# The order of the first 196 tasks of a fused conditioned-block kernel

## The chip, the cores and the metric

The kernel runs on one core of a Trainium2 chip. The metric is the device time of one execution in microseconds (us): lower is better. A core has five engines that run side by side, each through its own list of instructions in order: PE (TensorE, matrix products), ACT (ScalarE), DVE (VectorE), POOL (GpSimd) and SP, which here does nothing but issue transfers. PEld in a profile is PE's loading of weights, DMA stands for the 16 DMA engines that move the data.

## The reference

A block with adaptive layer norm, linear attention ("hedgehog" features) and a gated MLP, on 2048 tokens of width 512, in bfloat16:

```python
mod = (_silu(c) @ w_mod)                     # six vectors of 512: sa, ca, ga, sb, cb, gb
h = _layernorm(x) * (1 + ca) + sa
qkv = h @ wqkv                               # 32 heads of 16
pq, pk = q @ w_phi, k @ w_phi                # a 16x16 matrix per head
phi_q = concat(softmax(pq), softmax(-pq));   phi_k likewise
kv = sum_s phi_k v;  z = sum_s phi_k
o = (phi_q kv) / (phi_q z + 1e-6)
x = x + ga * (o @ wo)
h = _layernorm(x) * (1 + cb) + sb
x = x + gb * ((sigmoid(h @ w_gate) * (h @ w_up)) @ w_down)      # width 1376
```

## The kernel before

The tokens are 16 tiles of 128. The kernel describes its whole work as some 1230 named tasks with their data dependences; each has one engine, or a choice of engines. A text, `ORDER`, names all tasks in the order in which they are emitted, with `@A`, `@D` or `@P` where a task is to run on ACT, DVE or POOL instead of the first engine of its choices. Every engine's list of instructions is this text, filtered for the engine. `arrange` walks the text once and gives each buffer (PSUM banks, tiles of x normalised, exponentials) the place that has been free the longest; a task that gets a place waits for the last reader of what stood there before. There is no scheduler at run time.

The names that matter here. `t` is a token tile, `g` a group of the first layer norm (group 0 is tile 0, group 1 tile 1, group 2 tiles 2 and 3, group 3 tiles 4 and 5, and so on), `j` a quarter of the width:

- `ld_x0a` ... `ld_wmm2`: loads, all issued by SP. `ld_x..` are token tiles, `ld_wk..` the key weights, `ld_wv0` the value weights, `ld_wm00a` ... `ld_wm01b` the modulation weights of sa and ca, `ld_wmga` those of ga, and `ld_wmm2` (L556, 1.5 MB) those of sb, cb and gb.
- `wqT0` to `wqT3` (L669): loads of a quarter of the query weights that transpose on the way. `xT1_t` (L736): the same from SBUF to SBUF for tiles 10 to 13.
- `warm..` (L600): products of zeros, whose result nobody reads, that keep PE at work; `warm0` has six, each of the others one.
- `c1`, `c2`, `c3`: the silu of c. `modc1.h` (L630, PE) and `modc1ch` (L635 on ACT or L638 on DVE): sa and ca by halves, product and copy. `modca` (L616, from `ld_wmga`): ga. `modc2.0`, `modc2.1` (L616, PE, from `ld_wmm2`): sb, cb and gb.
- `tpw`, `wTc`, `fold1k`, `foldc1k`: the key weights are transposed on PE, copied, multiplied by w_phi (L679) and copied again (L685), so that keys come out as features' arguments; `fold0k`, `foldc0k` the same for the queries, from `wqT`.
- `st1_t` (DVE), `rs1_g` (ACT as Ln and Exp, L709 and L710, or POOL, L712 and L713), `nmr1_g` (DVE, L718), `xn1_t` (POOL L731, ACT L727, tile 0 DVE L729): the first layer norm. `tphgj` (PE, L744) transposes a quarter, `hm1_gj` (ACT L751, DVE or POOL L753) modulates it on its way out of PSUM.
- `Kta`, `Ktb`, `Vta`, `Vtb`, `Qt` (PE, L817, L821, L871): products for keys, values, queries; `et`, `qet` (ACT, L776): exponentials; `nt` (DVE, L780): sums; `rt`: reciprocals (ACT as Ln and Exp, L794 and L795, or DVE, L798); `phit` (POOL or DVE, L787); `vat` (ACT or DVE, L836); `kvt` (PE, L282): adds the tile to the sums over the tokens.

The attention and the MLP follow in the same text. SP issues a load when it comes to it in its list; each load carries one of eight semaphores, and a load waits for the landing of the one eight places ahead.

Of the kernel before, what the change touches and what calls it, by code (L numbers as in the profile page):

```python
# [43 lines left out]
modc1c1 st1_8 ld_x3a warm1_8 K1a hm1_23 xn1_5 xn1_4 tph12 nmr1_6 st1_9 hm1_03@A hm1_13@A hm1_02@A ld_wv0 wqT3 xn1_10 xn1_11 rs1_5@P K0a K0b tph31 hm1_42@A
warm1_9 hm1_12@A hm1_22@A tph32 e0.0 K3a tph30 K3b hm1_30@A ld_wmga K1b tph33 warm1_10 tph40 st1_14 st1_15 st1_13 hm1_31@A hm1_32 wqT0 e3.0 wqT1 K2b hm1_40
nmr1_5 rs1_8@P n0.0 nmr1_8 hm1_33 e2.0 V0a V1a fold03 xn1_9 xn1_8 V1b V0b e1.0 n2.0 V2a V2b tph50 hm1_50 warm1_11 xn1_15 xn1_14 n1.0 V3a wqT2 fold00 fold01
tph43 r0.0@A va1 va0 phi0.0 foldc03 fold02 foldc01 foldc02 n3.0 st1_12 foldc00 xT1_10 xT1_11 r2.0 va2@D ld_wmm2 modca.0 modca.1 hm1_60@P hm1_63@P hm1_62@P
tph82 hm1_82@A r3.0@A modcac r1.0@A phi2.0@D phi1.0@D V3b K4a K4b rs1_7@P Q0 Q2 kv0.0 Q1 qe0.0 va3 qe2.0 hm1_43@A qe1.0 modc2.0 tph52 modc2.1 tph51 nmr1_7
xn1_12 xn1_13 phi3.0@D ld_wo qn0.0 modc2c e4.0 kv1.0 qn2.0 hm1_52 kv2.0 Q4 K5a kv3.0 xT1_12 xT1_13 qphi0.0@P qphi0.1@P qn1.0 qe4.0 qphi2.1 tph80 K5b hm1_80@A
hm1_51@A e5.0 pT0 qphi2.0 n4.0 r4.0@A qn4.0 n5.0 phi4.0@D qphi1.1@P hm1_61@P qphi1.0@P tph53 V5 K7a V4 va5 hm1_53@A V6 pT2 hm1_70@P qphi4.1 va4 hm1_71 mask4  # L50
va6 K6a K7b K6b e6.0 K8 tph83 hm1_83 r5.0 qphi4.0@P e8.0 pT1 pT4 ld_wd2 tph81 hm1_81 n6.0 n8.0 e7.0 n7.0 V7 kv4.0 hm1_72@P K11 K9 V9 K14 V8 r6.0@A e9.0 va7
va9 r7.0@A e11.2 e11.6 phi5.0 phi6.0 hm1_73@P n9.0 r9.0@A kv5.0 gwa gra gwb e11.4 e14.0 K10 phi7.0@D kv6.0 K12 V10 kv7.0 e14.4 r8.0 n11.6 n11.2 r11.6 phi9.0
e10.0 e12.0 ld_wd ld_wu0 grb n11.4 n14.0 r11.2 n14.4 r14.0 n10.0 r14.4@A phi8.0 va8 V11 V14 n12.0 e11.0 K13 n11.0 phi11.6 r11.4 wo1 r11.0 va10 r10.0@A va11
kv8.0 kv9.0 phi11.2@D phi11.0@D phi10.0@D phi11.4@D V12 K15 e13.0 wmod_free ld_wg0 phi14.4 phi14.0 kv10.0 kv11.4 kv11.6 Q6 kv11.0 e13.4 r12.0@A e15.4 n13.0
n13.4 r13.0 r13.4 n15.4 e15.0 va14 V15 V13 qe6.0 va12 kv11.2 n15.0 r15.0 r15.4@A va13 phi13.4 Q5 phi15.4 phi13.0@D va15 phi15.0@D phi12.0@D wo0 wo3 Q3 kv12.0
kv13.0 kv14.0 kv15.0 qn6.0 kvn0 kvz0 kv13.4 kv14.4 kv15.4 kvz1 kvn1 num0a num1a num2a wo2 rd0a wo_all rd1a qe3.0 u0a num0b num4a num1b rd0b Q11 qe5.0 rd2a u0b
u2a rd4a num2b qn3.0 u1a rd1b tpo0 Q8 qphi6.0@P qphi6.1@P oT0 out0 num4b rd2b u1b wd0 qe11.0 u2b qphi3.1@P qphi3.0@P x1_0 rd4b st2_0 qe8.0 Q7 qe7.0 tpo1 oT1
Q10 Q9 out1 Q15 oT2 rs2_0 qn5.0 nmr2_0 xn2_0 u4a u4b x1_1 qn7.0 tsw xnT0 out2 qphi5.1@P qphi5.0@P pT6 mod02 mod00 qphi7.0@P pT3 mod03@A mod01@A qe15.0
qphi7.1@P Q13 g0.8 x1_2 tg0.8 g0.1 st2_1 wd1 rs2_1 tg0.1 u0.8 u0.1 g0.0 num3b g0.4 hm0.1 hm0.8 pT5 qe9.0 tg0.4 g0.9 wd2 u0.4 u0.9 rd3b u3b tg0.9 g0.5 num3a
hm0.4 hm0.9 u0.2 u0.0 num6a tg0.5 tg0.0 rd3a u3a u0.5 g0.2 hm0.0 hm0.5 rd6a nmr2_1 qe10.0 tg0.2 oT4 g0.10 u0.10 wd6 hm0.2 g0.3 pT7 tg0.3 u6a g0.6 num6b u0.3  # L60
y0.0 y0.1 rd6b tg0.10 hm0.10 hm0.3 num5a num5b u6b rd5b wd3 wd4 wd5 oT3 oT6 xn2_1 qe13.0 tg0.6 rd5a y0.2 u5b g0.7 tg0.7 out4 u5a oT5 qn11.0 u0.6 u0.7 xnT1
num7a hm0.6 hm0.7 mod13@A mod12@A rd7a x1_4 y0.3 out3 qphi11.1@P qphi11.0@P x1_3 st2_3 out6 mod10@A mod11@A g1.2 tg1.2 g1.1 tg1.1 num7b wd7 u1.3 u1.2 hm1.2
u7a g1.4 u1.1 y0.4 rd7b hm1.1 u1.4 y0.5 tg1.4 hm1.4 g1.0 g1.10 u1.10 g1.3 u7b st2_2 rs2_2 tg1.10 tg1.3 hm1.10 hm1.3 pT11 out5 tg1.0 u1.7 g1.7 x1_6 nmr2_2 u1.0
hm1.0 g1.5 u1.5 x1_5 qn10.0 wd8 y0.6 g1.6 oT7 xn2_2 xn2_3 g1.8 y0.7 Q14 y0.8 wd10 tg1.7 tg1.5 hm1.5 out7 u1.8 u1.6 st2_4 tg1.6 xnT2 xnT3 wd9 x1_7 qphi10.0 Q12
hm1.7 st2_6 mod21@P mod20@P qphi10.1@P y1.0 pT10 tg1.8 mod22@A mod23@A hm1.6 g1.9 y1.1 y1.2 tg1.9 u1.9 y0.9 y1.3 y1.4 g2.5 y0.10 g2.6 st2_5 qe12.0 st2_7 hm1.8
qn9.0 tg2.5 qe14.0 rs2_4 hm1.9 rs2_3 nmr2_4 y1.5 u2.0 g2.1 g2.0 tg2.0 xn2_7@D hm2.0 nmr2_3 fin0 y1.6 g2.2 tg2.2 u2.6 u2.2 hm2.2 u2.1 num11b y1.7 g2.4 rd11b
u11b xn2_6@P xnT7 xnT6 u2.5 tg2.1 xn2_5 qphi9.1@P hm2.1 tg2.6 u2.8 xn2_4 hm2.5 g2.3 num11a rd11a u11a u2.9 qphi9.0@P xnT5 y1.8 xnT4 tg2.4 u2.4 hm2.4 hm2.6
tg2.3 g2.9 u2.3 hm2.3 g2.8 tg2.8 tg2.9 u2.7 mod41@P mod43@P mod32@P mod42@P mod31@P qn13.0 g2.10 hm2.8 g2.7 y1.9 num10a qn8.0 num10b y2.0 y1.10 tg2.7 hm2.7
rd10a hm2.9 qphi8.0@P u2.10 pT9 y2.1 y2.2 y2.3 y2.4 y2.5 qn14.0 num9b rd9b qphi13.0 qphi8.1@P mod30@A mod33@A tg2.10 mod40@A y2.6 y2.7 g3.3 wr qphi13.1@P
tg3.3 oT11 g3.0 u10a rd10b u10b pT8 oT10 hm2.10 qn15.0 g3.8 num9a rd9a u9a u3.0 out11 y2.8 g3.1 y2.9 qphi14.1 fin1 x1_11 u9b u3.3 hm3.3 st1 tg3.8 tg3.0 u3.8  # L70
num8a st2_11 num8b rd8b rd8a u8a pT13 qphi15.0 hm3.8 u8b u3.9 g3.4 u3.2 out10 x1_10 qphi14.0 oT8 oT9 hm3.0 st2_10 y2.10 g3.6 u3.6 qn12.0 rs2_6 out8 tg3.4
# [987 lines left out]
```

## Time and profile before

| What | Value |
|---|---|
| Time, median of 3 runs | 205.37 us (205.24 to 207.14) |
| Profiled execution: span from first to last instruction | 203.3 us |
| Outside the span, median less span | 2.1 us |
| Share of the span busy: PE, PEld, DVE, ACT, POOL | 96%, 52%, 79%, 52%, 50% |
| Mean granted PE clock | 1.00 |
| HBM read, written | 11.58 MB, 2.10 MB |

Of the profiled execution the page gives the span; what its whole time has beside the span is read from the median of the runs. A line of a profile in order of time has the start in us, the duration, engine, line of the kernel, operation, output and inputs by name, and how often it came in a row; in brackets, how long the engine had been idle and what ended that. SPq is SP's queue, where an issue is shown with the time that it took. The chain of waits is the work that ended last, followed backward.

### The profile page before, as it was taken

To read this page: it belongs to the slowest core of one execution; us is meant where nothing else is said; L and a number is where in the kernel's file an instruction comes from. 1 tells how busy PE (TensorE), PEld (TensorE's weight loads), DVE (VectorE), ACT (ScalarE), POOL (GpSimd) and SP (SyncE) were. 2 spreads that over 40 slices of the span, in tenths; PEclk is the share of its full clock that TensorE was granted. 3 is DMA by queue.
4 is the path that set the end of the run, shared out by engine and by line. 5 is a ranking of instruction groups with operands and counts; after the bars stand their busy time and mean duration, and the time that the engine had idled before them with its cause. 6 is when DMAs were issued, how large, how long until landed. Compare 5 with 4: busy or idle time off the path is not lost.

```text
span 203.3 us, 4138 instructions
## 1 busy us (share of the span) xinstructions
PE 194.9 (96%) x1447; PEld 106.7 (52%) x1471; DVE 160.6 (79%) x374; ACT 105.9 (52%) x257; POOL 102.1 (50%) x143
## 2 busy tenths in 40 slices
PE   7789999999999999999999999999999999999993
PEld 2455655555464687668844444444444444444442
DVE  3899999999999999999897797794969844326633
ACT  2799999999978984556451115212113311324100
POOL 4698977789689999767670056230030324000000
PEclk9999999999999999999999999999999999999999
...
GB/s 172 331 329 182 233 264 102 123 82 280 400 213 43 146 102 55 94 37 106 125 59 103 51 54 103 101 83 77 26 26 69 13 79 31 40 13 7 50 55 55
DMA packets 49453, 22.94 MB, mean 113 GB/s; under 512 B 38065, under 2 KB 47634, under 8 KB 49426
## 3 DMA queue, kind: packets, MB, share of 16 engines
...
HBM read 11.58 MB, written 2.10 MB: 67 GB/s over the span
## 4 chain that ended last, share of the span: by engine, by line
PE 75%; DVE 8%; ACT 4%; DMA 4%; issue 4%; POOL 3%; SPq 0%; POOLq 0%; DVEq 0%
PE y_ps L485 19%; PE u_ps L447 18%; PE g_ps L447 17%; PE a_ps L356 5%; DMA wmod_sb<-in_w_mod_dram 4%; PE k_ps L817 3%; PE warm L600 3%; DVE ks L780 3%; PE num L326 2%; POOL phi L787 2%; PE q_ps L871 2%; PE v_ps L821 2%; PE g_ps L449 1%; ACT h1T L751 1%; DVE qks L780 1%
## 5 line engine op out<-in xcount | busy, mean ns | idle before, releaser
L457 ACT ACTIVATE tg<-g_ps 128x512 bf16<-128x512 f32 (+5 forms) x66 | 28.8, 455 | 66.7 <-PE g_ps L447 39.5
L468 DVE SCALAR_TENSOR_TENSOR wmod_sb<-tg,u_ps 128x512 bf16<-128x512 bf16 (+4 forms) x63 | 30.3, 492 | 18.0 <-ACT tg L457 11.3
L485 PE MATMUL y_ps<-wd_sb,wmod_sb 128*128 128x512 bf16 (+4 forms) x180 | 44.2, 366 | 0.2
L447 PEld LDWEIGHTS <-wg_sb 128*128 128x128 bf16 (+1 forms) x252 | 21.9, 99 | 16.1 <-issue 0.2
L447 PEld LDWEIGHTS <-wu_sb 128*128 128x128 bf16 (+1 forms) x252 | 21.8, 99 | 16.0 <-issue 0.3
L784 POOL TENSOR_TENSOR qphi<-qe,qks 128x512 bf16<-128x512 bf16 x24 | 25.1, 1063 | 3.9 <-DMA pT<-qphi 1.0
L485 PEld LDWEIGHTS <-wmod_sb 128*128 128x128 bf16 (+1 forms) x187 | 17.1, 98 | 16.0 <-issue 0.6
L447 PE MATMUL u_ps<-wT_sb,wu_sb 128*128 128x512 bf16 (+2 forms) x124 | 23.8, 322 | 0.1
L447 PE MATMUL g_ps<-wT_sb,wg_sb 128*128 128x512 bf16 (+2 forms) x122 | 23.0, 321 | 0.2
L447 PE MATMUL g_ps<-wqk_sb,wg_sb 128*128 128x128 bf16 (+4 forms) x127 | 19.9, 286 | 0.1
L447 PE MATMUL u_ps<-wqk_sb,wu_sb 128*128 128x128 bf16 (+4 forms) x127 | 19.8, 286 | 0.2
L492 DVE TENSOR_TENSOR ot<-y_ps,x 128x512 bf16<-128x512 f32 (+2 forms) x17 | 11.1, 654 | 10.5 <-PE y_ps L485 10.4
L780 DVE TENSOR_REDUCE qks<-qe 128x64 bf16<-128x1024 bf16 x16 | 19.2, 1204 | 0.0
L780 DVE TENSOR_REDUCE ks<-e 128x64 f32<-128x1024 bf16 (+2 forms) x22 | 19.1, 905 | 0.0
L376 POOL TENSOR_SCALAR ve<-mv 128x2 f32<-128x2 f32 (+1 forms) x8 | 1.8, 226 | 34.2 <-DVE mv L366 34.1
L776 ACT ACTIVATE e<-k_ps 128x512 bf16<-128x512 f32 (+2 forms) x44 | 17.7, 504 | 0.1
L776 ACT ACTIVATE qe<-q_ps 128x512 bf16<-128x512 f32 x32 | 17.3, 608 | 0.8 <-POOL phi L787 0.4
L787 POOL TENSOR_TENSOR phi<-e,kr 128x1024 bf16<-128x1024 bf16 (+2 forms) x10 | 14.5, 1454 | 3.9 <-ACT kr L795 2.1
L817 PE MATMUL k_ps<-wqk_f,h1T 128*128 128x512 bf16 x61 | 15.9, 379 | 0.1
L356 PE MATMUL a_ps<-wo_sb,oT 128*128 128x512 bf16 x60 | 15.9, 379 | 0.2
L871 PE MATMUL q_ps<-wqk_f,h1T 128*128 128x512 bf16 x60 | 15.7, 379 | 0.2
L821 PE MATMUL v_ps<-wv_sb,h1T 128*128 128x512 bf16 x62 | 15.5, 379 | 0.0
...
## 6 DMA issues: line engine op xcount, KB each, us to landing
...
x_sb<-in_A_x_dram SPq DMA_DIRECT2D x6, 256.0 KB, 4.9
...
wu_sb<-in_B_w_up_dram SPq DMA_DIRECT2D x1, 1376.0 KB, 11.0
...
wmod_sb<-in_w_mod_dram SPq DMA_DIRECT2D x4, 256.0 KB, 6.0
wqk_sb<-in_A_wqkv_dram SPq DMA_DIRECT2D x2, 256.0 KB, 4.5
```

The costliest lines, as they stand in the source:

```text
L356: pe.matmul(ap_[:], lhsT=oT[:, j, :], rhs=wo_sb[:, j, :], start=(j == 0), stop=(j == KT - 1))
L447: pe.matmul(ps[:fsz, 0:n], lhsT=w[:, j, ft * P:ft * P + fsz], rhs=h[:, j, 0:n], start=(j == 0), stop=(j == KT - 1))
L457: G.add(f"tg{k}.{ft}", {"ACT": 0.13 + n * 0.00083}, lambda e, tg=tg, g_ps=g_ps, fsz=fsz, n=n: act.activation(tg[:fsz, 0:n], g_ps[:fsz, 0:n ...
L468: dve.scalar_tensor_tensor(hm_all[:fsz, hm[k].slot, ft, 0:n], tg[:fsz, 0:n], 1.0, u_ps[:fsz, 0:n], op0=ALU.add, op1=ALU.mult)
L485: mm = pe.matmul(y[:, 0:c1 - c0], lhsT=hm_all[:fsz, hm[k].slot, ft, tl * P:(tl + 1) * P], rhs=wd_sb[:fsz, ft, c0:c1], start=(ft == 0), sto ...
L776: act.activation(ee[:, a:b, s].rearrange("p g f h -> p g (f h)"), kp[:, a * 64:b * 64].rearrange("p (g n) -> p g n", n=64), ACT.Exp, scale ...
L780: dve.tensor_reduce(ks[:, a:b].rearrange("p g s h -> p (g s) h"), ee[:, a:b].rearrange("p g s f h -> p (g s) h f"), axis=AX.X, op=ALU.add)
L784: engine(e).tensor_tensor(ph[:].rearrange("p (g s f h) -> p g s f h", s=2, f=DH, h=4)[:, :, s], ee[:, :, s], ks[:, :, 1 - s].unsqueeze(2). ...
L787: engine(e).tensor_tensor(ph[:, a * P:b * P].rearrange("p (g f h) -> p g f h", f=DH, h=4), ee[:, a:b].rearrange("p g s f h -> p (g s) f h" ...
L817: pe.matmul(kp[:], lhsT=h1T[:, j, t * P:(t + 1) * P], rhs=wqk_f[:, j, D:2 * D], start=(j == 0), stop=(j == KT - 1))
L821: pe.matmul(vp[:], lhsT=h1T[:, j, t * P:(t + 1) * P], rhs=wv_sb[:, j, :], start=(j == 0), stop=(j == KT - 1))
L871: pe.matmul(qp[:], lhsT=h1T[:, j, t * P:(t + 1) * P], rhs=wqk_f[:, j, 0:D], start=(j == 0), stop=(j == KT - 1))
```

## The change

The text `ORDER` is changed up to `V3b`, the second half of the value product of tile 3: the first 196 tasks stand in another order, and 19 of them run on another engine. From `V3b` on, all 1034 tasks stand as they did, on the same engines. No task is added or taken away. The first two lines of the text:

```diff
-pmem ld_x0b wdz warm0 c1 warm1_0 warm1_1 bd st1_2 st1_3 warm1_2 warm1_3 c2 rs1_2 ld_x0a ld_wk0 warm1_4 tpw0 st1_0 rs1_0 wTc0 st1_1 ld_wk1 rs1_1 c3 xn1_0
-nmr1_1 nmr1_2 ld_x1b st1_6 st1_7 tpw1 tpw3 wTc3 wTc1 tpw2 fold10 foldc10 wTc2 ld_wm00b ld_x1a ld_wm00a tph00 fold11 fold13 rs1_4 foldc13 fold12 foldc12 xn1_3
...
+wdz pmem warm0 ld_x0a st1_1 rs1_1 st1_0 c1 c2 ld_x0b warm1_0 warm1_1 warm1_2 warm1_3 ld_wk0 ld_wk1 nmr1_1 xn1_1@A st1_3 warm1_4 st1_2 rs1_0 xn1_0 tph11 tpw1
+tpw0 ld_x1b ld_x1a wTc1 warm1_5 tpw2 ld_wm00b c3 tph10 tph03 tph00 st1_7 tpw3 bd rs1_2@P tph13 wTc0 nmr1_2 xn1_3 xn1_2 warm1_6 ld_wm00a st1_6 wTc2 st1_4 st1_5
...
```

The 19: `rs1_2` and `rs1_4` go from ACT to POOL and `rs1_6` from POOL to ACT; `xn1_1` from POOL to ACT; `hm1_21`, `hm1_23`, `hm1_32`, `hm1_40` and `hm1_50` from DVE to ACT, and `hm1_00`, `hm1_03`, `hm1_22` and `hm1_42` from ACT to DVE; `modc1c1` from ACT to DVE; `r0`, `r1` and `r3` from ACT to DVE and `r2` from DVE to ACT; `va2` from DVE to ACT. Tile 0 and 1 are now normalised ahead of tiles 2 and 3. All twelve single fillers `warm1_..` stand ahead of the first key product; before, four of them stood behind it.

SP's list, from the last small modulation load to the big one (`wmod_sb` 128x4x1536 is `ld_wmm2`, `wT_sb` are the `wqT`, `h1T` the two `xT1`), as one piece of the difference:

```order
 L537 DMA x_sb<-in_A_x_dram 128x2x512
+L669 DMA_TRANSPOSE wT_sb<-in_A_wqkv_dram 128x4x128
 L537 DMA x_sb<-in_A_x_dram 128x4x512
 L551 DMA wv_sb<-in_A_wqkv_dram 128x4x512
 L669 DMA_TRANSPOSE wT_sb<-in_A_wqkv_dram 128x4x128
 L555 DMA wqk_sb<-in_w_mod_dram 128x4x512
-L669 DMA_TRANSPOSE wT_sb<-in_A_wqkv_dram 128x4x128 x3
+L669 DMA_TRANSPOSE wT_sb<-in_A_wqkv_dram 128x4x128 x2
 L736 DMA_TRANSPOSE h1T<-xn 128x4x128 x2
 L556 DMA wmod_sb<-in_w_mod_dram 128x4x1536
```

One of the four transposing loads of the query weights (`wqT1`) now stands ahead of `ld_x3a`, `ld_wv0` and `ld_wmga`; the other loads ahead of `ld_wmm2` change places in pairs only.

ACT's list from the first copies of transposed key weights to the first modulated tiles. Before:

```order
L664 COPY wT_sb<-tp_w 128x4x128
L709 ACTIVATE ve_83<-mv_82,eps 128x1
L710 ACTIVATE rs_84<-ve_83 128x1
L664 COPY wT_sb<-tp_w 128x4x128 x2
L685 CAST wqk_f<-fold_ps 128x512
L664 COPY wT_sb<-tp_w 128x4x128
L709 ACTIVATE ve_83<-mv_82,eps 128x2
L710 ACTIVATE rs_84<-ve_83 128x2
L685 CAST wqk_f<-fold_ps 128x512 x3
L635 COPY modc<-modc_ps 128x2
L636 ACTIVATE modc<-modc_ps 128x2
```

Of the change:

```order
L709 ACTIVATE ve_83<-mv_82,eps 128x1
L710 ACTIVATE rs_84<-ve_83 128x1
L576 ACTIVATE c_ps<-c_ps 128x4
L727 ACTIVATE xn<-x_sb,nmr,rs_84 128x512
L664 COPY wT_sb<-tp_w 128x4x128 x4
L685 CAST wqk_f<-fold_ps 128x512 x4
L635 COPY modc<-modc_ps 128x2
L636 ACTIVATE modc<-modc_ps 128x2
```

The four copies (`wTc`) and the four casts (`foldc1`) now each follow one another with no layer-norm task between them, and `xn1_1` stands ahead of them.

ACT's list at the end of the changed part, from the value copies or the last sums of the keys to `qe0.0`, the first exponential of a query (L776 `qe`). Before:

```order
L836 CAST vaug_111<-v_ps 128x32x16
L685 CAST wqk_f<-fold_ps 128x512 x4
L751 ACTIVATE h1T<-tp_h,modc 128x256
L794 ACTIVATE ks<-ks 128x64
L795 ACTIVATE kr<-ks 128x64
L648 COPY gcol<-modc_ps 128x4
L794 ACTIVATE ks<-ks 128x64
L795 ACTIVATE kr<-ks 128x64
L776 ACTIVATE qe<-q_ps 128x8x64 x2
```

Of the change:

```order
L685 CAST wqk_f<-fold_ps 128x512 x2
L836 CAST vaug_111<-v_ps 128x32x16
L836 CAST vaug_112<-v_ps 128x32x16
L794 ACTIVATE ks<-ks 128x64
L795 ACTIVATE kr<-ks 128x64
L751 ACTIVATE h1T<-tp_h,modc 128x256 x2
L776 ACTIVATE qe<-q_ps 128x8x64 x2
```

One reciprocal (`r2`) is left there instead of two, with one value copy (`va2`) and one `hm1` more; the casts of the folded query weights stand further apart.

More of the change, by code (lines that the diff above doesn't have):

```diff
@@ L44 @@
[L44 to L71, printed above, removed]
@@ new lines @@
+tpw0 ld_x1b ld_x1a wTc1 warm1_5 tpw2 ld_wm00b c3 tph10 tph03 tph00 st1_7 tpw3 bd rs1_2@P tph13 wTc0 nmr1_2 xn1_3 xn1_2 warm1_6 ld_wm00a st1_6 wTc2 st1_4 st1_5
+wTc3 fold11 fold10 warm1_7 foldc11 ld_x2b fold13 warm1_8 st1_11 foldc10 fold12 warm1_9 foldc13 modc1.0 warm1_10 ld_wm01b tph20 foldc12 warm1_11 rs1_4@P nmr1_4
+ld_wm01a modc1c0 hm1_11@A hm1_10@A tph02 rs1_3@P tph01 tph23 hm1_20@A hm1_01@A st1_10 tph21 hm1_21@A hm1_00 modc1.1 modc1c1@D rs1_6 nmr1_3 tph22 tph12 ld_x2a
+wqT1 hm1_22 hm1_13@A hm1_03 xn1_7 K1a K0a hm1_02@A hm1_23@A xn1_6 tph42 tph40 xn1_5 hm1_40@A st1_8 tph41 ld_x3a xn1_4 K3a hm1_42 hm1_12@A ld_wv0 nmr1_6 tph43
@@ new lines @@
+K3b hm1_41@A xn1_11 tph30 xn1_10 st1_9 rs1_5@P hm1_30@A tph31 wqT3 tph32 K1b ld_wmga st1_15 st1_14 hm1_31@A fold01 foldc01 K0b tph33 wqT2 rs1_8@P K2a K2b
+hm1_33 nmr1_5 V0a wqT0 V0b V3a xn1_9 e3.0 V1a xT1_11 e0.0 fold03 n3.0 V1b nmr1_8 xn1_14 va0 e2.0 n0.0 st1_13 r0.0 modca.0 modca.1 xn1_15 st1_12 xn1_8 foldc03
+n2.0 modcac e1.0 hm1_32@A V2a fold02 phi0.0 n1.0 r1.0 fold00 V2b foldc02 foldc00 r3.0 va1 xT1_10 hm1_60@P ld_wmm2 va2 r2.0@A hm1_62@P tph82 hm1_82@A tph50
+phi2.0@D phi1.0@D hm1_50@A hm1_63@P V3b K4a K4b rs1_7@P Q0 Q2 kv0.0 Q1 qe0.0 va3 qe2.0 hm1_43@A qe1.0 modc2.0 tph52 modc2.1 tph51 nmr1_7 xn1_12 xn1_13
@@ new lines @@
+rd6b tg0.10 hm0.10 hm0.3 num5a num5b u6b rd5b wd3 wd4 wd5 oT3 oT6 xn2_1 qe13.0 tg0.6 rd5a y0.2 u5b g0.7 tg0.7 out4 u5a oT5 qn11.0 u0.6 u0.7 xnT1 num7a hm0.6
+hm0.7 mod13@A mod12@A rd7a x1_4 y0.3 out3 qphi11.1@P qphi11.0@P x1_3 st2_3 out6 mod10@A mod11@A g1.2 tg1.2 g1.1 tg1.1 num7b wd7 u1.3 u1.2 hm1.2 u7a g1.4 u1.1
+y0.4 rd7b hm1.1 u1.4 y0.5 tg1.4 hm1.4 g1.0 g1.10 u1.10 g1.3 u7b st2_2 rs2_2 tg1.10 tg1.3 hm1.10 hm1.3 pT11 out5 tg1.0 u1.7 g1.7 x1_6 nmr2_2 u1.0 hm1.0 g1.5
+u1.5 x1_5 qn10.0 wd8 y0.6 g1.6 oT7 xn2_2 xn2_3 g1.8 y0.7 Q14 y0.8 wd10 tg1.7 tg1.5 hm1.5 out7 u1.8 u1.6 st2_4 tg1.6 xnT2 xnT3 wd9 x1_7 qphi10.0 Q12 hm1.7
```

51 lines of the change are left out of this document (34 added, 17 removed).

## The prediction

> **What bounds the kernel now.** I read the page's totals first, then the busy time by stages, then the chain of waits, then each engine's instructions in order of time around the place where the change ends.
>
> ```profile
> span 203.3 us, 4138 instructions
> PE 194.9 (96%) x1447; PEld 106.7 (52%) x1471; DVE 160.6 (79%) x374; ACT 105.9 (52%) x257; POOL 102.1 (50%) x143
> 10.00:15.00 5.00, 4.29 (x59) 2.78 (x60) 4.83 (x17) 4.86 (x16) 4.68 (x9) 1.00 1.14 330
> 15.00:20.00 5.00, 4.95 (x31) 2.50 (x30) 4.62 (x16) 5.00 (x13) 4.39 (x9) 1.00 1.38 182
> 66.00:200.00 134.00, 133.00 (x891) 72.54 (x904) 99.68 (x233) 47.77 (x102) 49.33 (x67) 1.00 0.34 65
> ```
>
> The columns of a stage are its length and the busy time of PE, PEld, DVE, ACT and POOL, then PE's clock, the share of the DMA engines and GB/s. PE is taken from 15 us to the end (4.95 of 5, 133 of 134). A busy PE need not be a PE at its peak, so I looked at the spacing: a product of 512 columns follows the last one at 0.216 us.
>
> ```profile
> 33.35 0.86 PE v_ps L821 x4
> ```
>
> Four such products in 0.86 us is what every full row of PE between 16 and 200 us shows. So behind the head the kernel is one dense row of PE work in a fixed order, and its end moves with the moment at which PE gets through the head. In the tail nothing is reordered. The question is only: when does PE get past the seam, and what holds it there?
>
> ```profile
> 21.41 7.44 DMA wmod_sb<-in_w_mod_dram
> 28.90 0.82 PE modc_ps L616 x24
> ...
> 24.37 0.59 PE L821 MATMUL v_ps<-wv_sb,h1T 128*128 128x512 bf16 x2
> 27.65 1.02 PE L871 MATMUL q_ps<-wqk_f,h1T 128*128 128x512 bf16 x3
> 28.90 0.75 PE L616 MATMUL modc_ps<-sc_bf,wmod_sb 128*128 128x1 bf16 x22 [0.22 <-DMA wmod_sb<-in_w_mod_dram]
> ```
>
> The first two lines are of the chain of waits, the others of PE in order of time. The changed part ends with V3b at 24.37 (the first task that stays). From there PE runs K4, Q0, Q2, kv0 and Q1; Q1 starts at 27.65 and its four products end at 27.65 + 4 x 0.216 = 28.51 (one record is missing). Then comes modc2.0, which reads the 1.5 MB load wmm2. That load was issued at 21.41 and landed 7.44 us later, at 28.85; modc2.0 starts at 28.90. **PE has 0.39 us of true waiting there, and the chain leaves the engines for the DMA.** This load is the gate between head and tail.
>
> **The change part by part.**
>
> *PE reaches the gate earlier.* In the kernel before, four of the fillers (warm1_8 to warm1_11) stand behind the first key product; now all stand ahead of it. That takes 4 x 0.216 = 0.86 us out of the dense part.
>
> ```profile
> 10.30 0.55 PE L630 MATMUL modc_ps<-sc_bf,wmod_sb 128*128 128x1 bf16 x16
> 13.56 0.54 PE L630 MATMUL modc_ps<-sc_bf,wmod_sb 128*128 128x1 bf16 x16
> 14.20 0.38 PE L817 MATMUL k_ps<-wqk_f,h1T 128*128 128x512 bf16 x1
> 5.63 2.08 SPq L542 DMA_DIRECT2D wmod_sb<-in_w_mod_dram  x2
> wmod_sb<-in_w_mod_dram SPq DMA_DIRECT2D x4, 256.0 KB, 6.0
> 10.48 1.54 ACT L685 CAST wqk_f<-fold_ps 128x512 bf16<-128x512 f32 x3
> 11.90 0.18 ACT L635 COPY modc<-modc_ps 128x2 f32<-128x2 f32 x1
> 12.19 2.42 ACT L751 ACTIVATE h1T<-tp_h,modc 128x128 bf16<-128x128 bf16 x6
> 14.48 0.18 ACT L635 COPY modc<-modc_ps 128x2 f32<-128x2 f32 x1
> ```
>
> The first key product stands at about 14.0 (14.20 is the second of the pair). modc1.0 is done at 10.85, but ACT copies the modulation columns only at 11.90, because three copies of folded weights go first, from 10.48 on. In the new order ACT has the four weight casts behind it by about 10.7: xn1_1 has come to it (I take 0.6 us, as one of its 512-column casts above), one rs task less stands ahead, and its copies of the transposed weights run without a break. So the modulation copy can start at 10.95, 0.95 us earlier. The second modulation product, at 13.5 so far behind other PE work, then runs when its weights land: the last of the two issues from 5.63 starts at about 6.7, and 6.0 us later is 12.7. Its columns go to DVE now, and with 0.6 us for the product, the copy and one hm1 the first key product comes at about 13.6. PE arrives at the gate 0.4 + 0.86 = 1.26 us earlier, at **27.3** instead of 28.51.
>
> *ACT and DVE at the seam.* From the first modulation copy (11.90) to qe0.0 (26.73) ACT is full for 14.83 us.
>
> ```profile
> 18.01 1.06 ACT L751 ACTIVATE h1T<-tp_h,modc 128x256 bf16<-128x256 bf16 x2
> 18.90 3.09 ACT L776 ACTIVATE e<-k_ps 128x512 bf16<-128x512 f32 x6
> 21.77 0.37 ACT L794 ACTIVATE ks<-ks 128x64 f32<-128x64 f32 x1
> 22.34 1.06 ACT L836 CAST vaug<-v_ps 128x512 bf16<-128x512 f32 x2
> 23.28 2.06 ACT L685 CAST wqk_f<-fold_ps 128x512 bf16<-128x512 f32 x4
> 26.73 1.08 ACT L776 ACTIVATE qe<-q_ps 128x512 bf16<-128x512 f32 x2
> 28.10 0.33 DVE L718 TENSOR_SCALAR nmr<-mv,rs 128x1 f32<-128x1 f32 x2
> 38.68 0.41 DVE L753 TENSOR_SCALAR h1T<-tp_h,modc 128x256 bf16<-128x256 bf16 x1 [0.38 <-PE tp_h L744]
> ```
>
> Prices are from start to start: an hm1 of two tiles 0.45 (18.01 to 18.90 for two), of one tile 0.35 (six mixed ones from 12.19 to 14.48 take 2.29), a reciprocal as Ln and Exp 0.57 (21.77 to 22.34), a value copy 0.47 (22.34 to 23.28 for two). In that stretch ACT gains five wide hm1 (21, 23, 32, 40, 50), one rs (0.44), r2 and va2, and gives up two wide (22, 42) and two narrow (00, 03) hm1, modc1c1 (0.29) and r0, r1, r3: 3 x 0.45 - 2 x 0.35 + 0.44 - 0.29 - 2 x 0.57 + 0.47 = +0.1. With some 0.2 of new short waits ACT is at qe0.0 at 10.95 + 14.83 + 0.3 = 26.1 to 26.2, 0.5 earlier. DVE does the mirror image of it (a net of about zero) and loses the waits that it has ahead of 20 us; I put its seam (28.10) 0.4 earlier. POOL gets two rs tasks for one rs and one xn, about even. None of the three reaches the seam late, and none of the leads is worth much: DVE waits 0.38 us for PE at 38.68 in any case.
>
> *The gate itself.* This term decides. The queue of loads holds the same transfers ahead of wmm2; wqT1, a transposing load, goes from behind the ga weights to a place ahead of x3a, and wv0, wqT3 and the ga weights each start one transfer later.
>
> ```profile
> 10.47 1.78 SPq L669 DMA_TRANSPOSE wT_sb<-in_A_wqkv_dram  x1
> 12.92 5.08 SPq L669 DMA_TRANSPOSE wT_sb<-in_A_wqkv_dram  x3
> 18.12 3.23 SPq L736 DMA_TRANSPOSE h1T<-xn  x2
> 14.54 3.03 POOL L731 TENSOR_SCALAR xn<-x_sb,rs,nmr 128x512 bf16<-128x512 bf16 x4
> 17.00:18.00 1.00, 1.00 (x9) 0.54 (x7) 0.97 (x4) 1.00 (x3) 0.92 (x3) 1.00 1.15 349
> 18.50:19.00 0.50, 0.50 (x7) 0.37 (x6) 0.41 (x2) 0.50 (x3) 0.42 (x3) 1.00 0.01 1
> 19.00:19.50 0.50, 0.50 (x6) 0.25 (x3) 0.34 (x2) 0.50 (x3) 0.50 (x1) 1.00 0.08 9
> 22.50:23.00 0.50, 0.45 (x3) 0.24 (x3) 0.50 (x3) 0.50 (x2) 0.50 (x2) 1.00 0.88 74
> 24.00:25.00 1.00, 1.00 (x18) 0.66 (x16) 1.00 (x2) 1.00 (x3) 1.00 (x2) 1.00 1.05 418
> ```
>
> SP is full from 10.47 to 21.98: issuing is the pace, and the transposes take 1.3 to 1.8 us each. The last two, xT1_10 and xT1_11, read what POOL finished at 14.54 + 3.03 = 17.57, ahead of 18.12, so they did not wait for data; in the new order I get the same two xn at about 17.2. So the work ahead of wmm2 is the same on SP and on the DMA engines, and I take its landing as unchanged: **28.85, term 0**. The bounds: below, the issue could come so early that the hole around 22.5 to 23.5 closes (74 GB/s against 418 later; 1.0 us at a fifth of the rate is 0.8 us): -0.8. Above, a transpose among plain loads can leave a hole as at 18.5 to 19.5, where 1 and 9 GB/s moved: +1.0, and wqT1 now stands alone among plain loads, so one more such place exists. Zero lies between the two.
>
> [...]
>
> *Late loads inside the head.* x3a and wv0 land later by about one transpose, which I put at 1 us (4 transposes and two plain loads fill SP from 10.47 to 18.0). V0a would come at 18.2 and wv0 at 17.5 to 18; fold02 and fold00 may wait up to 0.8 us for wqT2 and wqT0. The 1.55 us between 27.3 and 28.85 cover that.
>
> *The sum.* At the gate: max(27.3, 28.85) = the same 28.85 as now. PE's lead of 1.26 us turns into a longer wait for the load, 1.55 instead of 0.39 us. Behind it one other wait can shrink a little by DVE's lead:
>
> ```profile
> 58.57 0.93 PE L326 MATMUL num<-kvb,pT 128*128 128x68 bf16 x24 [0.36 <-DVE kvb L299]
> ```
>
> I give it 0.1 us. The profiled span would be 203.3 - 0.1 = 203.2. The median of the timed runs, 205.37, lies 2.1 above the profiled span; with that the forecast is **205.3 us**. A difference under 1% (2.05 us) is about what a measurement of this kernel cannot tell from no change.
>
> **The rivals.**
>
> *The load lands earlier (faster).* If SP gets to wmm2 early enough, the gate moves to 28.05, and if the holes between transposes go too, down to PE's own 27.3. For it: the holes are there. Against: SP is full, and nothing is taken off it. Time: 205.3 - 0.8 to 205.3 - 1.55, so 203.8 to 204.5. PE's own arrival is a floor, so a gain of over 1% would need PE's head to shrink by more than I find. [...]
>
> *The load lands later (slower).* The lone transpose ahead of x3a leaves a hole of its own and the three behind keep theirs. Each us of delay behind 28.85 costs one us of the whole, since PE is dense after it: one hole, 1.0 us, gives 206.3; two give 207.3. It is slower from the first tenth that wmm2 lands behind 28.85, and over 1% from 30.9 on. For it: the 1 GB/s at 18.5 begins where a plain load gives way to transposes. Against: between 10 and 15 us the engines moved 330 GB/s with small packets too.
>
> *The clock.* PE ran its first fillers at half rate:
>
> ```profile
> 4.11 2.31 PE L600 MATMUL warm<-wd_sb 128*128 128x512 bf16 x5
> ```
>
> Five in about 2.1 us is 0.43 each, though the clock column says 1.00. Were PE to fall back to that between 10.8 and 13.6 because fillers moved ahead, each product behind would take 0.43. The slack of 1.55 us covers seven such products, at 0.216 more each; fourteen, a stretch of 6 us, would cost 3.0 - 1.55 = 1.5 and give 206.8. [...]
>
> **How the numbers follow.** Gate unchanged within 0.6 us: 0.66 (204.7 to 205.9). Load earlier: 0.14. Load later: 0.15. Clock, or a head that is late for a reason I have not priced: 0.05. The range that holds eight of ten takes in most of both load rivals: 203.9 to 206.8. Faster by over 1% (under 203.3) needs PE's floor to be wrong: 0.04. Slower by over 1% (over 207.4) needs two holes or a late head: 0.07. The rest, 0.89, is the same.
>
> **What would show it.** In the changed profile: modc2.0 still ends a wait for wmm2 on PE, starting at 28.3 to 29.5; Q1's products end about 1.2 us earlier than 28.51, at 27.0 to 27.9; the first modulation copy on ACT stands near 11.0; qe0.0 near 26.2; no filler behind the first key product; wmm2 issued at 20.8 to 21.9. If PE reaches modc2.0 after the load has landed, my head is wrong; if the load lands outside 28.0 to 29.9, my term 0 is; if the two agree and the time still differs by over 1%, then the tail isn't a rigid row of PE work, and that reading is wrong.

## The result and the profile after

| | Before | After |
|---|---|---|
| Time, median | 205.41 us (17 executions) | 204.08 us (17 executions) |
| Ratio, 95% interval | | 0.992 [0.9898, 0.9942] |
| Profiled execution: span | 203.3 us | 202.6 us |

The change makes the kernel 0.8% faster: 204.08 us lies in the range of 203.9 to 206.8, but the forecast was no change, at 205.3, and the interval excludes that. A ratio leaves out executions more than 1.5% above the fastest of their kernel (one of 714.59 us among them); medians and counts below take all but that one.

The changed kernel, from the page (totals, the chain by engine) and from PE in order of time:

```profile
span 202.6 us, 4159 instructions
PE 69%; DVE 14%; ACT 6%; issue 3%; POOL 3%; DMA 3%; SPq 1%; DVEq 0%; POOLq 0%
...
13.22 0.55 PE L630 MATMUL modc_ps<-sc_bf,wmod_sb 128*128 128x1 bf16 x16 [0.48 <-ACT h1T L751]
13.84 1.02 PE L817 MATMUL k_ps<-wqk_f,h1T 128*128 128x512 bf16 x4
...
26.75 1.02 PE L871 MATMUL q_ps<-wqk_f,h1T 128*128 128x512 bf16 x4
27.68 0.82 PE L616 MATMUL modc_ps<-sc_bf,wmod_sb 128*128 128x1 bf16 x24
```

modc2.0 (L616) starts at 27.68 instead of 28.90 and no longer ends a wait for the DMA; wmm2 has left the chain. SP's queue shows why, and one group row gives the time from issue to landing:

```profile
9.28 1.51 SPq L669 DMA_TRANSPOSE wT_sb<-in_A_wqkv_dram  x1
12.01 1.62 SPq L669 DMA_TRANSPOSE wT_sb<-in_A_wqkv_dram  x1
14.30 3.07 SPq L669 DMA_TRANSPOSE wT_sb<-in_A_wqkv_dram  x2
17.49 3.13 SPq L736 DMA_TRANSPOSE h1T<-xn  x2
20.67 0.58 SPq L556 DMA_DIRECT2D wmod_sb<-in_w_mod_dram  x1
wmod_sb<-in_w_mod_dram SPq DMA_DIRECT2D x1, 1536.0 KB, 6.8
```

The six transposing loads take SP 1.51 + 1.62 + 3.07 + 3.13 = 9.33 us; before they took 1.78 + 5.08 + 3.23 = 10.09. wmm2 is issued 0.74 us earlier, about as much. (SP's other issues differ too, but nearly cancel: it is done with the last small modulation load 0.64 us later, at 8.35, and the plain loads behind that take 0.72 us less.) It lands 6.84 us later, at 27.51 (before: 28.85), while Q1's products end at 27.61. **The load came 1.34 us earlier and PE 0.90 us; now PE is the later of the two.**

From there the tail doesn't keep all of it: modc2.0 is 1.22 us earlier, the sums over the tokens from 45 us on 0.9, the span 0.7. And the medians differ by more than the spans, 1.33 us. Both differences needed an explanation.

### The profile page after: what moved, and what is told of

The parts are those of the page before. It is cut to its first block, busy times and chain, and to the rows that moved or that the text cites. A ratio compares the mean times of both kernels' runs of the same rounds, so it can differ in the third digit from the quotient of the medians.

```text
span 202.6 us, 4159 instructions
## 1 busy us (share of the span) xinstructions
PE 195.7 (97%) x1471; PEld 106.2 (52%) x1471; DVE 160.4 (79%) x375; ACT 106.1 (52%) x252; POOL 102.8 (51%) x144
## 4 chain that ended last, share of the span: by engine, by line
PE 69%; DVE 14%; ACT 6%; issue 3%; POOL 3%; DMA 3%; SPq 1%; DVEq 0%; POOLq 0%
PE y_ps L485 19%; PE u_ps L447 18%; PE g_ps L447 17%; DVE ks L780 7%; PE a_ps L356 6%; DMA wqk_sb<-in_A_wqkv_dram 3%; PE num L326 2%; DVE kr L798 2%; ACT qe L776 2%; DVE phi L787 2%; PE q_ps L871 1%; PE g_ps L449 1%; ACT h1T L751 1%; DVE qks L780 1%; POOL phi L787 1%
## 5 line engine op out<-in xcount | busy, mean ns | idle before, releaser
L485 PE MATMUL y_ps<-wd_sb,wmod_sb 128*128 128x512 bf16 (+4 forms) x187 | 45.7, 367 | 0.0
L492 DVE TENSOR_TENSOR ot<-y_ps,x 128x512 bf16<-128x512 f32 (+2 forms) x17 | 11.1, 654 | 10.2 <-PE y_ps L485 10.1
L776 ACT ACTIVATE e<-k_ps 128x512 bf16<-128x512 f32 (+2 forms) x44 | 18.2, 522 | 0.0
L776 ACT ACTIVATE qe<-q_ps 128x512 bf16<-128x512 f32 x32 | 17.4, 618 | 0.6 <-POOL phi L787 0.4
L817 PE MATMUL k_ps<-wqk_f,h1T 128*128 128x512 bf16 x64 | 16.5, 379 | 0.0
L821 PE MATMUL v_ps<-wv_sb,h1T 128*128 128x512 bf16 x64 | 16.1, 379 | 0.1
```

Source lines behind the costliest of these rows:

```text
L485: mm = pe.matmul(y[:, 0:c1 - c0], lhsT=hm_all[:fsz, hm[k].slot, ft, tl * P:(tl + 1) * P], rhs=wd_sb[:fsz, ft, c0:c1], start=(ft == 0), sto ...
L776: act.activation(ee[:, a:b, s].rearrange("p g f h -> p g (f h)"), kp[:, a * 64:b * 64].rearrange("p (g n) -> p g n", n=64), ACT.Exp, scale ...
L817: pe.matmul(kp[:], lhsT=h1T[:, j, t * P:(t + 1) * P], rhs=wqk_f[:, j, D:2 * D], start=(j == 0), stop=(j == KT - 1))
L821: pe.matmul(vp[:], lhsT=h1T[:, j, t * P:(t + 1) * P], rhs=wv_sb[:, j, :], start=(j == 0), stop=(j == KT - 1))
```

## The experiments

### Load order and fillers, one at a time

Two rivals to "the gate opens at the later of PE and the load": the load alone carries the gain, or PE's head and the moved engines do. Each of the two parts was put alone into the kernel before, then both, and the load was put back in the changed kernel.

The load alone:

```diff
-ld_x3a ... ld_wv0 wqT3 ... ld_wmga ... wqT0 e3.0 wqT1
+wqT1 ld_x3a ... ld_wv0 wqT3 ... ld_wmga ... wqT0 e3.0
```

> The kernel before with one task moved: the transposing load wqT1 ahead of ld_x3a, nothing else. Theory M (the gate opens at the later of two arrivals, PE's and the load's): the 1.5 MB load wmm2 is issued about 20.7 instead of 21.41 and lands at 27.5 to 28.1 instead of 28.85; PE's own arrival stays at 28.51, so modc2.0 starts at about 28.55 with no wait for the load, and the time is 0.3 to 0.4 us lower: about 205.0 against 205.4. Rival L (the load alone carries the gain): 1.3 us lower, 204.1. Rival P (PE's head and the engines alone carry it): no change, 205.4.

The fillers alone (twelve as before, the last four now behind tph00, fold13 and tph11):

```diff
-tph00 fold11 fold13 ... tph11 ... warm1_5 ... warm1_6 ... warm1_7 ... K2a ... warm1_8 K1a ... warm1_9 ... warm1_10 ... warm1_11
+tph00 warm1_5 warm1_6 fold11 fold13 warm1_7 ... tph11 warm1_8 ... warm1_9 ... warm1_10 ... warm1_11 ... K2a ... K1a
```

> The kernel before with only the four fillers that stand behind the first key product moved ahead of it, into PE's waits between 7.8 and 11.6 us; loads and engines as they were. Theory M: Q1's products end at about 27.65 to 27.9 instead of 28.51, the load still lands at 28.85, modc2.0 still starts at 28.9 after a wait of 1.0 to 1.2 us; time within 0.1 of 205.4. Rival P: 0.86 us lower, 204.5. Rival L: no change.

Both, with no task on another engine:

> The kernel before with both edits: wqT1 ahead of ld_x3a, and the four fillers ahead of the first key product. No task changes its engine. Theory M: modc2.0 starts at the later of 27.65 to 27.9 (PE) and 27.5 to 28.1 (load), so 27.7 to 28.1, 0.8 to 1.2 us earlier than 28.90; time 204.2 to 204.6, most of the changed kernel's gain. Rival L: 204.1, the same as with the load order alone. Rival P: 204.5, the same as with the fillers alone. If it stays at 205.0 or more, the moved engines and the rest of the order matter too.

The load put back in the changed kernel:

```diff
-ld_x2a wqT1 ... wqT3 ... ld_wmga ... fold01 foldc01 ... fold02
+ld_x2a ... wqT3 ... ld_wmga wqT1 ... fold01 foldc01 fold02
```

> The changed kernel with wqT1 put back behind ld_wmga (and the fold product that reads it moved behind that of fold03), all else as changed. Theory M: the load lands at 28.6 to 28.9 again, PE arrives at 27.6 and waits 1.0 to 1.3 us at modc2.0, which starts at about 28.8; time 205.2 to 205.4. Rival P: the gain stays, 204.1. Rival L: the gain is gone, 205.4, as in theory M.

Times against the kernel before on the same chip (205.53 us, 35 executions):

| | Median | Ratio, 95% interval |
|---|---|---|
| Load order alone | 205.32 | 0.9977 [0.9944, 1.0010] |
| Fillers alone | 205.23 | 0.9992 [0.9955, 1.0030] |
| Both | 204.04 | 0.9927 [0.9899, 0.9955] |
| Changed kernel, load put back | 205.05 | 0.9987 [0.9949, 1.0025] |

By the median, neither alone is worth anything that can be measured; together they give the whole gain of the change, without one task on another engine, so the moved engines and the rest of the new order need not add anything. Neither edit by itself gives what the two give, and in the changed kernel the median's gain is mostly lost with the load put back.

That isn't yet max(PE, load), since these medians mix executions at full clock with slower ones, as the next section shows. At full clock, the load order alone is 0.63 us faster than the kernel before (four executions: 204.24, 204.30, 204.46 and 205.76, against 205.01), the fillers alone 0.07 us (eight), both 0.98 us (twelve), and the changed kernel with the load put back still 0.47 us (eight). So the rival that the load alone carries the gain falls only for the median: between executions at full clock it has most of it, as far as four of them can tell. The fillers missed their expectation in the profile: Q1's products end at 28.37, 0.14 us earlier than before (0.5 us counted from the early loads, as below), and not at 27.65 to 27.9. What the fillers bring is, as far as these runs show, the clock more than an earlier PE.

SP's queue and PE's start of modc2.0, for the fillers alone, for both, and for the load put back, in this order:

```profile
13.25 5.05 SPq L669 DMA_TRANSPOSE wT_sb<-in_A_wqkv_dram  x3
21.72 0.57 SPq L556 DMA_DIRECT2D wmod_sb<-in_w_mod_dram  x1
29.14 0.82 PE L616 MATMUL modc_ps<-sc_bf,wmod_sb 128*128 128x1 bf16 x24 [0.61 <-DMA wmod_sb<-in_w_mod_dram]
```

```profile
13.56 3.09 SPq L669 DMA_TRANSPOSE wT_sb<-in_A_wqkv_dram  x2
20.07 0.57 SPq L556 DMA_DIRECT2D wmod_sb<-in_w_mod_dram  x1
28.03 0.82 PE L616 MATMUL modc_ps<-sc_bf,wmod_sb 128*128 128x1 bf16 x24
```

```profile
12.26 5.08 SPq L669 DMA_TRANSPOSE wT_sb<-in_A_wqkv_dram  x3
20.57 0.59 SPq L556 DMA_DIRECT2D wmod_sb<-in_w_mod_dram  x1
27.76 0.82 PE L616 MATMUL modc_ps<-sc_bf,wmod_sb 128*128 128x1 bf16 x24 [0.27 <-DMA wmod_sb<-in_w_mod_dram]
```

In these profiles PE waits for the load with three query transposes in a row, and with two it doesn't. The times of single profiles mislead here (the load put back seems early, at 27.7), because the early loads come up to 1.2 us sooner or later from one execution to the next: the last small modulation load landed between 12.14 (the load put back) and 13.35 (the second profile of the changed kernel), although SP's list is the same in the two up to it. Counted from that landing, the big load lands after:

| Kernel | us |
|---|---|
| Before; fillers alone | 16.05; 15.92 |
| Changed kernel, load put back | 15.58 |
| Load order alone; both | 14.76; 15.18 |
| Changed kernel; its second profile | 14.33; 14.45 |

So the place of wqT1 brings some 0.9 us, between 0.7 and 1.3 by the pairs of this table. The other 0.5 us in the changed kernel (issue to landing 6.84 instead of 7.44) has a cause that no run separates.

### The time that the profiles don't show: PE's clock

In the load order's single profile PE arrived late, at 29.24, though no wait is shown. The page's row of the granted clock and four stages (the third number from the right is the clock):

```profile
PEclk9969999999999999999999999999999999999999
...
11.00:12.00 1.00, 0.79 (x18) 0.66 (x16) 0.96 (x3) 0.97 (x4) 1.00 (x2) 0.90 1.17 304
12.00:13.00 1.00, 0.94 (x3) 0.20 (x2) 0.96 (x3) 0.99 (x3) 0.92 (x3) 0.50 1.87 221
...
14.00:15.00 1.00, 1.00 (x23) 0.97 (x22) 0.88 (x3) 0.81 (x4) 1.00 (x2) 0.50 1.07 317
15.00:16.00 1.00, 0.89 (x5) 0.30 (x4) 0.86 (x4) 1.00 (x3) 1.00 (x3) 0.89 1.10 347
```

From 11.80 to 15.22 PE had half its clock: 3.42 us. The mean clock of each execution is recorded, and it falls into three groups: 0.996 and above, 0.989 to 0.992, and 0.983 or 0.984. One window of 3.42 us at half rate in a span of 203.5 is a mean of 0.9916, two are 0.983. Executions by windows, as their mean clock tells them (a profiled one at 0.990 and one at 0.991 show one, a profiled one at 0.983 shows two), with the median time of each group:

| Kernel | None | One | Two |
|---|---|---|---|
| Before, all 104 executions beside the experiments | 30: 205.02 | 43: 205.55 | 31: 206.70 |
| Changed, both measurements | 27: 204.06 | 1: 205.76 | 0 |
| Load order alone | 4: 204.38 | 6: 205.31 | 2: 206.53 |
| Fillers alone | 8: 204.94 | 4: 206.99 | 0 |
| Both | 12: 204.03 | 0 | 0 |
| Changed, load put back | 8: 204.54 | 4: 206.71 | 0 |

**Between executions at full clock the change is worth 0.96 us (1.16 on the one chip where the clocks of both kernels are on record, 205.10 to 203.94); the rest of the median's gain is windows at half clock that hardly occur any more.** The profile of before happened to have none. A window does not cost the same everywhere: in the kernel before, the group with one is 0.53 us longer than that with none and the second adds 1.15, while with the fillers ahead one costs 2.05 to 2.17. That the wait at the gate hides part of a loss in the head would explain it in part, but no run shows it.

The table suggests two places: the head (windows in both kernels that have fillers behind the first key product) and the gate (windows in both whose fillers are ahead and whose load is late). Three runs test that here, and a fourth, with the reader moved, stands further down.

The gate filled: Q1's products done twice, so that PE works while it waits.

```diff
-            for j in range(KT):
+            for j in list(range(KT)) * (2 if t == 1 else 1):
                 pe.matmul(qp[:], lhsT=h1T[:, j, t * P:(t + 1) * P], rhs=wqk_f[:, j, 0:D], start=(j == 0), stop=(j == KT - 1))
```

> The kernel before with the four fillers ahead (as in the run of the fillers alone), and Q1's four products done twice, so that PE works through most of its wait for wmm2. Loads as before. Theory C (a wait of PE of about 1 us, in the head or at the gate, now and then lets the granted clock fall to half for about 3.5 us, which costs about 2 us): no execution with a mean clock under 0.995 is left; all times lie between 204.1 and 205.9, median 205.0; in the profile modc2.0 starts when the load lands, 28.7 to 29.1. Rival H (the low clock comes from the thin PE work in the head, whatever happens at the gate): as with the fillers alone, a third of the executions at a mean clock of 0.992 and 206.6 to 207.4.

205.39 us (204.86 to 206.03), ratio 0.9973 [0.9945, 1.0001]; all twelve executions at 0.997 and above, where the fillers alone had four of twelve below. The 0.86 us of useless products bring the upper end down from 207.35 to 206.03. On the clock theory C is borne out. On the time it isn't: 205.0 was expected, and at full clock this kernel is 0.46 us slower than the fillers alone. In its profile the second set of products ends at 29.01, 0.17 us after the load has landed.

The wait made longer: the fillers alone, with wo's load ahead of wmm2.

```diff
-ld_wmm2 ... ld_wo
+ld_wo ld_wmm2
```

> The kernel before with the four fillers ahead, and the load of wo ahead of wmm2, so that wmm2 is issued some 0.5 us later and lands 1.0 to 1.5 us later (29.9 to 30.6). Theory M: PE waits 1.7 to 2.3 us at modc2.0, and executions at full clock take 1.0 to 1.5 us more than with the fillers alone (204.9): 205.9 to 206.4. Theory C: more executions fall to a mean clock of 0.992 than the third with the shorter wait, half or more, each some 2 us longer, up to 208.5. Rival: no more of them than before, or none.

208.32 us, ratio 1.0121 [1.0089, 1.0153]; six of six with a window. None was left at full clock, so M's figure for those isn't tested. The profile caught one (PE's wait, then stages):

```profile
29.95 0.82 PE L616 MATMUL modc_ps<-sc_bf,wmod_sb 128*128 128x1 bf16 x24 [1.91 <-DMA wmod_sb<-in_w_mod_dram]
28.00:29.00 1.00, 0.04 (x1) 0.00 (x0) 1.00 (x2) 1.00 (x3) 0.82 (x2) 1.00 0.44 165
29.00:30.00 1.00, 0.05 (x2) 0.05 (x3) 1.00 (x2) 1.00 (x3) 0.75 (x1) 1.00 0.02 9
31.00:32.00 1.00, 1.00 (x37) 1.00 (x34) 1.00 (x2) 0.41 (x4) 0.00 (x0) 0.97 0.46 87
32.00:33.00 1.00, 0.78 (x9) 0.44 (x7) 0.48 (x1) 0.88 (x2) 0.97 (x1) 0.50 0.53 41
34.00:35.00 1.00, 1.00 (x9) 0.49 (x7) 0.00 (x0) 0.96 (x2) 0.10 (x1) 0.50 0.00 0
35.00:36.00 1.00, 1.00 (x13) 0.75 (x11) 0.65 (x2) 0.58 (x2) 0.00 (x0) 0.82 0.71 141
```

PE stood idle for 1.9 us; the clock fell 2 us after PE was busy again, at 31.94, and came back at 35.36. Between 32 and 35 us PE is busy for 0.78 to 1.00 of each us at the half rate, so an estimate is 3.42 / 2 = 1.7 us on top of the wait; with the fillers alone the two groups lie 2.05 us apart.

The fillers put back in the changed kernel:

```diff
-fold13 warm1_8 fold12 warm1_9 modc1.0 warm1_10 ... tph20 ... warm1_11 ... K1a ... K3a ... K1b ... V2b
+fold13 fold12 modc1.0 ... tph20 ... K1a warm1_8 ... K3a warm1_9 ... K1b warm1_10 ... V2b warm1_11
```

> The changed kernel with the last four of its twelve fillers put back behind the first key products, where the kernel before had them; loads and engines as changed. Theory C (PE's waits between 8 and 13 us let the granted clock fall to half for some 3.5 us in many executions; the fillers ahead prevent that): half or more of the executions show a mean clock of 0.983 to 0.992, and the median rises by 0.7 to 1.5 us, to 204.8 to 205.5; executions at full clock are at 204.0 to 204.4 (the four fillers cost PE 0 to 0.3 us). Rival (the fillers only cost PE time): clocks stay at 0.996 to 1.00, median 204.1 to 204.4.

206.37 us in the median of all twelve (204.8 to 205.5 was expected). Four executions at full clock: 204.12, the same as the changed kernel (on other chips), so four executions show no cost of the fillers' place to PE. Five with one window: 206.41; three with two: 207.58. The profiled one, with its two stages in which the clock changes:

```profile
PEclk9975999999999999999999999999999999999999
12.00:13.00 1.00, 0.57 (x5) 0.25 (x3) 0.96 (x5) 1.00 (x4) 0.92 (x3) 0.97 1.96 245
19.00:20.00 1.00, 1.00 (x8) 0.70 (x7) 0.71 (x2) 0.33 (x1) 0.92 (x3) 0.62 2.91 133
```

The half rate lasts from 12.94 to 19.76, 6.82 us or two windows of 3.41, where PE works on its first keys and values. Without four fillers in PE's waits ahead of 13 us the changed kernel's gain over the kernel before on the same chip (205.71) is gone: the ratio, which leaves out two of the twelve, is 0.9987 [0.9949, 1.0025]. The sums of the stages from 8 to 13 us show how thin PE's work is there, in the kernel before and in the changed one with all its fillers:

```profile
sum 5.00, PE 3.17 PEld 2.03 DVE 4.83 ACT 4.74 POOL 4.19; mean PE 0.63 PEld 0.41 DVE 0.97 ACT 0.95 POOL 0.84
```

```profile
sum 5.00, PE 4.40 PEld 2.38 DVE 4.66 ACT 4.68 POOL 3.54; mean PE 0.88 PEld 0.48 DVE 0.93 ACT 0.94 POOL 0.71
```

The windows that three profiles show last 3.41 to 3.42 us, and the same kernel has none, one or two in an execution. What sets one off no run shows: four of twelve executions had one where the profile shows a wait of 0.61 us at the gate (the fillers alone), and all six where it shows 1.91 us (wo's load ahead).

### Moving the reader, and a shorter head

The gate can be taken away by moving its reader:

```diff
-qe1.0 modc2.0 tph52 modc2.1 tph51 ... qn0.0 modc2c ... K5b ... e5.0
+qe1.0 tph52 tph51 ... qn0.0 ... K5b modc2.0 modc2.1 ... e5.0 modc2c
```

> The kernel before with the four fillers ahead, all loads in the old order, and the reader of the big load moved instead of the load: modc2.0 and modc2.1 behind the second key product of tile 5, the copy behind e5.0, some 6 us later. Theory M: the gate is gone, PE goes on from Q1 at 27.9 to 28.4, and the time is 204.1 to 204.4 as with load order and fillers together, with no execution under a mean clock of 0.995. Rival L (the new load order itself brings the gain, by something else than the gate): the time stays at 205.0 and above.

204.93 us, ratio 0.9949 [0.9918, 0.9981]; all at 0.996 and above, and full-clock executions hardly better than before's 205.02. Theory M in this form fails: the windows go with the wait, but not the time. PE in order of time, behind Q1, at Q4 and at modc2:

```profile
28.21 0.39 PE L744 MATMUL tp_h<-ident,xn 128*128 128x128 bf16 x4
29.25 1.02 PE L871 MATMUL q_ps<-wqk_f,h1T 128*128 128x512 bf16 x4
31.65 1.48 PE L616 MATMUL modc_ps<-sc_bf,wmod_sb 128*128 128x1 bf16 x48
```

Behind Q1 PE goes on at 28.21, where before modc2.0 started at 28.90, so it is 0.69 us ahead; at 33.0, with modc2 behind it in both kernels, it is 0.08 us ahead (32.99 against 33.07). It loses 0.31 us ahead of Q4 and 0.31 ahead of modc2.0; the profile doesn't name what ended these two waits. That modc2 filled such waits where it stood before is a reading that no run separates.

The changed kernel again:

> The changed kernel once more, as a control on the chip of these runs: 204.1, all mean clocks 0.996 to 1.00. Theory M with C: no execution above 205. In the profile PE reaches modc2.0 within 0.2 us of the landing of wmm2.

203.99 us, ratio 0.9919 [0.9886, 0.9951]; one of twelve at 0.992 (205.76). The median is as expected, the rest not quite: one execution had a window, and one at full clock took 205.31, so not every one stays under 205. In the profile PE reaches modc2.0 at 27.91, the load lands at 27.80.

The changed kernel with the reader moved in the same way, and with K1a ahead of modc1.1:

```diff
-modc1.1 ... tph22 tph12 ... K1a
+K1a modc1.1 ... tph22 tph12
```

> The changed kernel with two moves: the first key product K1a ahead of modc1.1 (PE waited 0.64 us there for the last modulation load, K1a takes 0.43), and modc2.0 and modc2.1 later, as in the run that moves the reader. Theory M (PE's head is the bound behind the gate): PE comes 0.4 us earlier past Q1, and the time falls to 203.6 to 203.8. Rival D (DVE is the bound between 28 and 58 us, as its larger share in the chain of waits says): 0 to 0.1 us of it stay, 204.0 to 204.1.

205.26 us, ratio 0.9967 [0.9935, 0.9998]: both expectations missed, it is 1.3 us slower than the control, and one of twelve has a window. PE in order of time:

```profile
13.13 0.59 PE L817 MATMUL k_ps<-wqk_f,h1T 128*128 128x512 bf16 x2 [0.18 <-ACT h1T L751]
28.52 0.27 PE L744 MATMUL tp_h<-ident,xn 128*128 128x128 bf16 x2 [0.21 <-ACT vaug L836]
29.50 1.02 PE L871 MATMUL q_ps<-wqk_f,h1T 128*128 128x512 bf16 x4 [0.20 <-ACT qe L776]
```

K1a itself waits for ACT, which delays modc1.1, and between 28 and 32 us PE waits for ACT three times: 0.21 us at 28.52, 0.20 at 29.50 and 0.15 at 31.90. The two edits weren't separated.

### Who takes 0.3 us of PE's lead

Work is taken off DVE:

```diff
-                dve.bn_stats(st1[:, t, :], x_sb[:, t, :])
+                dve.bn_stats(st1[:, t, :], x_sb[:, t, 0:(64 if t in (12, 13) else D)])
```

> The changed kernel with the layer-norm statistics of tiles 12 and 13 taken over 64 of the 512 columns: that leaves out part of the computation and takes about 1.1 to 1.2 us off DVE ahead of the seam, nothing off the other engines. Rival D (DVE takes 0.3 us of PE's lead between 28 and 58 us): PE keeps its whole lead, the tail shifts by another 0.2 to 0.3 us, 203.7 to 203.8. Theory A (ACT, which stands at qe0.0 only 0.17 us earlier than before, holds PE as well): 0 to 0.1 us, 203.9 to 204.1.

203.98 us, ratio 0.9900 [0.9872, 0.9927], all six at full clock. That is no gain that can be told from the changed kernel's 203.99 to 204.08, which however ran on other chips. It doesn't clear DVE either. DVE was 0.9 us earlier at 23.7 us but lost that again at nmr1_7, which it reached too early for POOL's rs1_7. That task in the changed kernel, and in this run:

```profile
28.14 0.34 DVE L718 TENSOR_SCALAR nmr<-mv,rs 128x1 f32<-128x1 f32 x2
28.28 0.33 DVE L718 TENSOR_SCALAR nmr<-mv,rs 128x1 f32<-128x1 f32 x2 [0.60 <-POOL rs L713]
```

So from 28 us on DVE had no lead in this run, and rival D stands untested: in the changed kernel DVE's list goes on from 28.14 to 43.6 with no wait shown, and the wait of 0.38 us for PE at 38.68 that the kernel before has is gone.

And, with that, work moved from ACT to DVE:

```diff
-va1 ... va2
+va1@D ... va2@D
```

> The changed kernel with the statistics of tiles 12 and 13 over 64 columns (part of the computation left out, 1.1 us off DVE) and the value copies va1 and va2 on DVE instead of ACT, so that about 0.9 us goes from ACT to DVE and DVE is about even. Theory A (ACT, at qe0.0 at 26.56, holds PE between 28 and 38 us, so that only 0.9 of PE's 1.2 us is kept): qe0.0 comes 0.6 to 0.9 us earlier and the time falls by 0.2 to 0.4 us, to 203.6 to 203.8. Rival B (no single engine holds it: what one gives up the next one takes, POOL's layer-norm tasks and the banks among them): within 0.1 us of the changed kernel, 203.9 to 204.1.

204.43 us, ratio 0.9938 [0.9909, 0.9967]: 0.4 us above the changed kernel's times, on a chip on which that one wasn't timed, although qe0.0 came 0.97 us earlier than in the profile of after (the small loads of that execution were 0.8 us earlier, too). PE then waited for the value copy, which holds a bank:

```profile
26.19 1.02 PE L871 MATMUL q_ps<-wqk_f,h1T 128*128 128x512 bf16 x4 [0.64 <-DVE vaug L836]
```

Theory A is not borne out, but the run doesn't settle it either, since the move brought a wait of its own. What takes the 0.3 us stays open; DVE from 28 us on, together with POOL's rs1_7 ahead of it, is a candidate that no run has excluded. From the start of modc2.0 to the last instruction it is 174.4 us before, 174.1 with both edits, 174.3 in the changed kernel with the load put back, and 174.9 and 175.0 in the two profiles of the changed kernel, in which modc2.0 comes earliest behind the small loads. No version tried beats the changed kernel by more than the chips differ; the kernel before with two edits (load order and fillers) equals it.

## Why the prediction was wrong

- **Term 0, the landing of wmm2, failed.** The forecast took it as unchanged at 28.85, because "the work ahead of wmm2 is the same on SP". It came 1.34 us earlier, and 1.6 to 1.7 against the early loads; the bound of -0.8 was too narrow. The same transposes aren't the same work: six of them took 9.3 to 9.5 us in the new order of loads and 9.9 to 10.1 in the old, in the profiles of before, after and the first four experiments. Of the four query transposes, those that follow another directly take 1.27 us in both orders. The one behind the ga weights takes 2.46 us in the old order and 1.75 in the new, the one with plain loads on both sides 1.78 and 1.51 to 1.62; why is not shown. I saw the row of 5.08 us and read only holes in it.
- The form of the sum, max(PE, load), held: in every profile that keeps modc2.0 in its place it starts right behind the later of the two. Its sizes didn't, since the load order alone gives more, and the fillers less, than PE's priced arrival says.
- The rival "the load lands earlier", at 0.14, was the case, with its floor at PE's arrival, as it said. That its time (203.8 to 204.5) holds 204.08 is partly luck: at full clock the change is worth 0.96 us, and the rest comes from the clock, which that rival didn't have.
- PE's arrival: 27.3 predicted, 27.61 measured. Its parts were worse than the whole. The fillers, put at 0.86 us, cost nothing that can be seen at full clock (204.12 against 204.06); they stood in waits.
- The first key product (13.6; 13.84), the first modulation copy (10.95; 11.35) and qe0.0 (26.2; 26.56) came later, since the small loads landed 0.4 to 0.5 us later in that execution. The 13.6 is also not what its parts add up to: 12.7 and 0.6 are 13.3, and PE did take up the key product 0.62 us behind the start of the modulation product, at 13.22. DVE's seam wasn't 0.4 earlier but even: 28.14.
- The clock rival was sought on the wrong side. It is real, but it belonged to the kernel before, which loses it: one window costs 0.5 us there, two 1.7. The hint was in the times: 207.14 beside 205.24. "Span plus 2.1 us" set the span of one execution against the median of others; time less span is 1.7 to 1.9 in every single execution with its span on record.
- The rigid tail held but for 0.3 us of 1.2 by 45 us, and 0.5 by the end.
